# State-times-W1 with two batches in one matmul, its result copied out of PSUM in two halves of 64 partitions

## The chip, the cores and the metric

The kernel runs on one core of one Trainium2 chip. The metric is the device time of one execution in microseconds. TensorE appears in the profile as PE, its weight loads as PEld, VectorE as DVE, ScalarE as ACT, GpSimd as POOL and SyncE as SP.

## The reference

Eight batches of eight heads, 512 positions of 64 values each, are attended to in both directions against a state of 32 rows per head; the result, 544 rows of 512 values per batch, goes through a mixture of eight experts with dense routing. Cut to what matters:

```
scores  = x @ state^T / 8          # softmax over the 32 state rows
xread   = softmax(scores) @ state  # 512 rows per head
sread   = softmax(scores2) @ x     # 32 rows per head, scores2 over the positions
x       = concat(xread, sread)     # 8 batches * 544 rows = 4352 rows of 512
P       = exp(x @ w_gate - max)    # then 8 rounds of row and column scaling
for e in range(8):
    h   = relu(x @ w1[e])          # 512 -> 1024
    out += P[:, e] * (h @ w2[e])   # 1024 -> 512
```

## The kernel before

**Factoring.** For the 512 xread rows of a batch the kernel does not form xread. It keeps the normalised softmax `AT` (for each batch 2 head quads `q` of 128 rows: 4 heads of 32 state rows) and uses `xread @ w1 = A @ (state @ w1)`. So for each batch and expert it first makes `G = state @ w1` (`state_times_w1`, line 210), of 2 quads times 1024 columns, and then `hps = G^T AT` (`layer1`, line 267). The 256 sread rows of all batches are kept as `xs` and go through `w1` directly (line 281).

**State times W1.** `stT_bd` (lines 67 and 133 to 136) holds the transposed state: for each batch and quad 128 columns, of which the 64 of one head pair (`par` 0 or 1) are one stationary operand. The contraction is over the 128 values of a head pair (64 of each of its two heads, block diagonal). A step (q, fh) makes 512 columns of G for one quad with two matmuls of 64 stationary columns each, the even pair into PSUM partitions 0 to 63, the odd one into 64 to 127, and then one copy of 128 partitions into `G` (line 221): on DVE for expert 0, on ACT for the others. There are 4 steps (2 quads, 2 halves of F) for a batch.

**Layer 2.** For expert 0 it is a plain matmul (line 293) whose result ACT copies to `acc` (line 296). For experts 1 to 7 it is a Strassen-Winograd product (`layer2_winograd`, line 304): seven block products per tile on PE (line 333, tiles `ra`, `rb`, `rc`), four sums of hT on DVE in front (lines 316 to 319, tile `sm`), seven scaled additions into `acc` on DVE (line 339), and four differences of W2 blocks for each expert on DVE (`w2_sums`, lines 110 to 113, tile `wt`). `wt` lies in the weight pool of the expert's parity, so two experts' `wt` can live at once.

**Order.** The framework lays out each engine's queue before the program runs, from the order of the source as priority and from what is ready in its own model; an engine then runs its queue in that order. So instructions of neighbouring steps are mixed, and expert 0's work lies among the attention's. In the source, expert 0 runs batch by batch: the four steps for the next batch's G, then the eight `layer1` steps, then four `layer2` steps. Experts 1 to 7 run by pairs of batches `j`: the list `second` (layer 2 of the pair before, 16 steps) is merged with `first` (layer 1 of this pair, 16 steps, with the 4 G steps of a following batch in one lump after the fourth step of each batch). The last pair of an expert has 8 more layer-1 steps for `xs`, and its layer 2, with 4 more steps, is merged into the first pair of the next expert. `w2_sums(e)` stands in the source ahead of that merge.

**Buffers.** PSUM has four banks for attention and four for the experts until expert 0 is done, then eight for the experts. `G` has 2 buffers (one a batch), `hT` 4, `sm` 2.

Of the kernel before, what the change touches and what calls it, by code (L numbers as in the profile page):

```python
# [11 lines left out]
FP16 = mybir.dt.float16  # L12
# [6 lines left out]
def kernel(  # L19
# [9 lines left out]
    nc = tc.nc  # L29

    B, H, S, D = x.shape
# [21 lines left out]
    mh = ctx.enter_context(tc.tile_pool(name="moe_h", bufs=4))  # L53
    mhs = ctx.enter_context(tc.tile_pool(name="moe_hs", bufs=1))
    gsb = ctx.enter_context(tc.tile_pool(name="gate_sb", bufs=2))
    gp = ctx.enter_context(tc.tile_pool(name="gp", bufs=2))

# [6 lines left out]
    Gg = persist.tile([128, B * NQ, E], FP16, name="Gg")  # L64
    Pmat = persist.tile([128, NTB, E], FP32, name="Pmat")
    acc = persist.tile([128, NTB, Dm], FP32, name="acc")
    stT_bd = persist.tile([128, B * NQ, 128], FP16, name="stT_bd")

    w1r = moe_w1.rearrange("e (kc p) f -> e p kc f", p=128)
    w2r = moe_w2.rearrange("e (fb p) d -> e p fb d", p=128)  # L70
# [33 lines left out]

    def w2_sums(e, w2h):

        wt = mw[e % 2].tile([128, 4, FH, DH], FP16, name="wt", tag="wt")
        b11, b12 = w2h[:, :FH, :DH], w2h[:, :FH, DH:]
        b21, b22 = w2h[:, FH:, :DH], w2h[:, FH:, DH:]
        nc.vector.tensor_sub(wt[:, 0], b12, b11)  # L110
        nc.vector.tensor_sub(wt[:, 2], b22, b12)
        nc.vector.tensor_sub(wt[:, 1], b22, wt[:, 0])
        nc.vector.tensor_sub(wt[:, 3], b21, wt[:, 1])
        return wt
# [17 lines left out]
    for g in range(2):  # L132
        t_ps = psA.tile([128, 8, 128], FP16, name="t_ps", tag="a")
        for j in range(8):
            nc.tensor.transpose(t_ps[:, j, :], st_bd[:, 8 * g + j, :], identh)
        nc.vector.tensor_copy(out=stT_bd[:, ds(8 * g, 8), :], in_=t_ps)

    x_nats += [load_x(1), load_x(2)]

    def attention(b):  # L140
        xn = x_nats[b]
        for q in range(NQ):
            bq = b * NQ + q
            xT_ps = psA.tile([128, 2, S], FP16, name="xT_ps", tag="a")
            for par in range(2):
                for sc in range(NSC):
                    nc.tensor.transpose(xT_ps[:, par, ds(128 * sc, 128)],  # L147
                                        xn[:, 2 * q + par, sc, :, :], identh)
            xT = asb.tile([128, 2, S], FP16, name="xT", tag="xT")
            nc.vector.tensor_copy(out=xT, in_=xT_ps)  # L150
            sc_ps = psA.tile([128, S], FP32, name="sc_ps", tag="a")
            for par in range(2):
                nc.tensor.matmul(sc_ps[ds(64 * par, 64), :],  # L153
                                 stT_bd[:, bq, ds(64 * par, 64)], xT[:, par, :])
            E2 = asb.tile([128, S], FP16, name="E2", tag="E2")
            rowsum = asb.tile([128, 1], FP32, name="rowsum", tag="rowsum")
            nc.scalar.activation(out=E2, in_=sc_ps, func=AF.Exp, scale=inv_sqrt_d,
                                 accum_out=rowsum)
            den_ps = psA.tile([128, S], FP32, name="den_ps", tag="a")
            nc.tensor.matmul(den_ps, headones, E2)  # L160
            lnd = asb.tile([128, S], FP32, name="lnd", tag="lnd")
            nc.scalar.activation(out=lnd, in_=den_ps, func=AF.Ln)
            rcp = asb.tile([128, S], FP16, name="rcp", tag="rcp")
            nc.scalar.activation(out=rcp, in_=lnd, func=AF.Exp, scale=-1.0)
            rrec = asb.tile([128, 1], FP32, name="rrec", tag="rrec")
            nc.vector.reciprocal(out=rrec, in_=rowsum)
            En = asb.tile([128, S], FP16, name="En", tag="En")
            nc.vector.tensor_scalar(out=En, in0=E2, scalar1=rrec, scalar2=None, op0=ALU.mult)
            ET_ps = psA.tile([128, NSC, 128], FP16, name="ET_ps", tag="a")
            for sc in range(NSC):  # L170
                nc.tensor.transpose(ET_ps[:, sc, :], En[:, ds(128 * sc, 128)], identh)  # L171
            ET = asb.tile([128, NSC, 128], FP16, name="ET", tag="ET")
            nc.vector.tensor_copy(out=ET, in_=ET_ps)
            nc.vector.tensor_mul(AT[:, q, ds(b * S, S)], E2, rcp)
            su_ps = psA.tile([128, 2, 64], FP32, name="su_ps", tag="a")
            for par in range(2):
                for sc in range(NSC):
                    nc.tensor.matmul(su_ps[:, par, :], xn[:, 2 * q + par, sc, :, :],
                                     ET[:, sc, ds(64 * par, 64)],
                                     start=(sc == 0), stop=(sc == NSC - 1))  # L180
            for i in range(2):
                nc.vector.tensor_copy(
                    out=xs[ds(64 * i, 64), ds(2 * q, 2), ds(b * Ns, Ns)],
                    in_=su_ps[ds(64 * i, 64), :, ds(32 * i, 32)])
# [15 lines left out]
    def state_times_gate():  # L200
        gg_ps = psA.tile([128, B * NQ, E], FP32, name="gg_ps", tag="a")
        for b in range(B):
            for q in range(NQ):
                for par in range(2):
                    nc.tensor.matmul(gg_ps[ds(64 * par, 64), b * NQ + q, :],
                                     stT_bd[:, b * NQ + q, ds(64 * par, 64)],
                                     wgh[:, 2 * q + par, :])
        nc.vector.tensor_copy(out=Gg, in_=gg_ps)

    def state_times_w1(b, w1h, e):  # L210

        evac = nc.vector.tensor_copy if e == 0 else nc.scalar.copy
        G = gp.tile([128, NQ, F], FP16, name="G", tag="G")

        def step(q, fh):
            g_ps = ps["m"].tile([128, 512], FP32, name="g_ps", tag="m")
            for par in range(2):
                nc.tensor.matmul(g_ps[ds(64 * par, 64), :],  # L218
                                 stT_bd[:, b * NQ + q, ds(64 * par, 64)],
                                 w1h[:, 2 * q + par, ds(512 * fh, 512)])  # L220
            evac(out=G[:, q, ds(512 * fh, 512)], in_=g_ps)  # L221

        return G, [partial(step, q, fh) for fh in range(F // 512) for q in range(NQ)]

    for b in range(B):
        if b + 3 < B:
# [7 lines left out]
    actx.close()  # L234
    mw[1] = ctx.enter_context(tc.tile_pool(name="moe_w1", bufs=1))
    sp = ctx.enter_context(tc.tile_pool(name="moe_s", bufs=2))

    for it in range(8):
        rsum = gsb.tile([128, NTB], FP32, name="rsum", tag="rsum")
# [47 lines left out]
    def layer2(e, c, hT, w2h):  # L287

        def step(tk):
            t = c * NSC + tk  # L290
            yps = ps["m"].tile([128, Dm], FP32, name="yps", tag="m")
            for fb in range(NFB):
                nc.tensor.matmul(yps, hT[:, fb, ds(tk * 128, 128)], w2h[:, fb, :],  # L293
                                 start=(fb == 0), stop=(fb == NFB - 1))
            if e == 0:
                nc.scalar.copy(out=acc[:, t, :], in_=yps)
# [73 lines left out]

        return [f for i in range(n) for f in tile_steps(i)]


    w1h, w2h = w_cur
    G_cur, steps = state_times_w1(0, w1h, 0)
    for f in steps:
        f()
    second = []
    for c in range(B + 1):
        if c == 3:  # L380
            w_nxt = load_w(1)
        steps = []
        if c + 1 < B:
            G_nxt, steps = state_times_w1(c + 1, w1h, 0)
        hT, st1 = layer1(c, w1h, G_cur)
        for f in steps + st1:
            f()
        second += layer2(0, c, hT, w2h)
        if c < B - 1:
            for f in second:  # L390
                f()
            second = []
        G_cur = G_nxt

    def merge(a, b):

        k = 0
# [5 lines left out]
        for f in b[k:]:  # L403
            f()

    psctx.close()
    ps["m"] = ctx.enter_context(tc.tile_pool(name="psW", bufs=8, space=bass.MemoryType.PSUM))

    G_nxt, gsteps = state_times_w1(0, w_nxt[0], 1)
    for f in gsteps:
        f()
    for e in range(1, E):
        w1h, w2h = w_nxt
        wt = w2_sums(e, w2h)
        for j in range(B // 2):
            last = j == B // 2 - 1
            first, hs = [], []
            for c in (2 * j, 2 * j + 1):  # L420
                G_cur = G_nxt
                hT, l1 = layer1(c, w1h, G_cur)
                hs.append(hT)
                gs = []
                if c + 1 < B:
                    G_nxt, gs = state_times_w1(c + 1, w1h, e)
                elif e + 1 < E:
                    G_nxt, gs = state_times_w1(0, w_nxt2[0], e + 1)
                first += l1[:4]
                if gs:  # L430
                    first.append(lambda gs=gs: [f() for f in gs])
                first += l1[4:]
            if last:
                hTs, l1 = layer1(B, w1h, None)
                first += l1
# [47 lines left out]
```

## Time and profile before

| | us |
|---|---|
| median of 3 runs | 848.27 (848.17 to 850.55) |
| the profiled execution | 847.74 |
| its span, first to last instruction | 846.0 |
| PE busy in the span | 809.3 |
| DVE busy | 615.7 |
| ACT busy | 474.9 |
| one expert's period in the steady part (from 258.34 to 353.65) | 95.31 |

The profiled execution is 1.7 us longer than its span, which is what lies ahead of the first instruction and behind the last. The first 20 us load x and state; attention with expert 0 runs to about 161 us; then come seven experts; the last 23 us are the last layer 2 and the stores. Matmuls are pipelined and their ends are modelled, so that the busy time of PE counts some waiting; the pieces of the chain of waits, which follow one another without overlap, tell what a group of matmuls adds to the time.

### The profile page before, as it was taken

Reading aid. Unit: us, or ns where it says so; the run is one execution under the profiler, and the core shown is the slowest. Engines: PE = TensorE matmul, PEld = TensorE weight load, DVE = VectorE, ACT = ScalarE, POOL = GpSimd, SP = SyncE. Lnnn points to the kernel's source line nnn. Section 1 sums busy time; section 2 is a strip of 40 time slices with the busy share of each in tenths; the row PEclk is TensorE's granted clock in tenths of the full one; section 3 lists DMA queues with packets and bytes.
Section 4 is the critical chain, followed back from the end, with each engine's and each line's share of the span. In section 5 each row is a group of like instructions: output and inputs, shape, how many; then the busy total and the mean of one; then the engine's idle time right before and its main releaser. Section 6 shows DMA issues by size and latency. Waiting matters only on the chain.

```text
span 846.0 us, 14483 instructions
## 1 busy us (share of the span) xinstructions
PE 809.3 (96%) x5840; PEld 511.3 (60%) x5840; DVE 615.7 (73%) x1320; ACT 474.9 (56%) x908; POOL 41.3 (5%) x67
## 2 busy tenths in 40 slices
PE   0899979999999999999999999999999999999997
PEld 0444434556676666766676666766676666766673
DVE  2656668458777877888777877888777877787763
ACT  0466635775565556555565556555565556555550
POOL 2322010000000000000000000000000000000000
PEclk9999999999999999999999999999999999999999
DMA  9630060330003300230002300230002300002223
GB/s 213 185 101 26 1 100 1 51 51 1 1 1 51 52 1 1 51 50 2 1 1 50 52 1 1 50 51 2 1 1 51 52 1 1 1 13 92 97 97 127
DMA packets 28900, 35.53 MB, mean 42 GB/s; under 512 B 4001, under 2 KB 20385, under 8 KB 28833
## 3 DMA queue, kind: packets, MB, share of 16 engines
q0 software_dynamic: 13328, 16.79, 12.5%
q1 hardware_dynamic: 15504, 17.83, 6.4%
q8 instruction: 45, 0.74, 0.4%
q14 instruction: 23, 0.18, 0.1%
HBM read 42.48 MB, written 8.91 MB: 61 GB/s over the span
## 4 chain that ended last, share of the span: by engine, by line
PE 91%; DVE 4%; DMA 2%; issue 1%; ACT 1%; SPq 0%; POOL 0%; POOLq 0%
PE hps L276 26%; PE ra L333 25%; PE rc L333 12%; PE g_ps L218 8%; PE yps L293 7%; PE rb L333 6%; PE hps L281 3%; DMA x_st<-in_x_dram 2%; DMA w2h<-in_moe_w_dram 1%; DVE G L221 1%; PE sc_ps L153 1%; PE xT_ps L147 1%; DVE xT L150 1%; PE den_ps L160 0%; PE ET_ps L171 0%
## 5 line engine op out<-in xcount | busy, mean ns | idle before, releaser
L283 ACT ACTIVATE hT<-hps 128x512 f16<-128x512 f32 (+1 forms) x576 | 315.4, 577 | 229.8 <-PE hps L276 202.7
L276 PE MATMUL hps<-AT,G 128*128 128x512 f16 x1024 | 286.0, 379 | 3.2 <-DVE G L221 2.1
L339 DVE SCALAR_TENSOR_TENSOR acc<-ra,Pmat,acc 128x256 f32<-128x256 f32 x456 | 216.5, 482 | 51.9 <-PE ra L333 50.8
L333 PEld LDWEIGHTS <-sm 128*128 128x128 f16 x1824 | 173.6, 98 | 77.3 <-issue 9.7
L333 PEld LDWEIGHTS <-hT 128*128 128x128 f16 x1368 | 129.6, 98 | 56.9 <-issue 25.2
L339 DVE SCALAR_TENSOR_TENSOR acc<-rc,Pmat,acc 128x256 f32<-128x256 f32 x228 | 109.9, 482 | 63.9 <-PE rc L333 62.9
L221 ACT CAST G<-g_ps 128x512 f16<-128x512 f32 x224 | 115.6, 599 | 46.0 <-PE g_ps L218 46.0
L333 PE MATMUL ra<-wt,sm 128*128 128x256 f16 x912 | 136.9, 273 | 0.0
L276 PEld LDWEIGHTS <-G 128*128 128x128 f16 x1024 | 98.6, 98 | 58.7 <-issue 14.1
L293 PE MATMUL yps<-w2h,hT 128*128 128x512 f16 x352 | 87.3, 385 | 0.0
L218 PE MATMUL g_ps<-w1h,stT_bd 128*64 128x512 f16 x512 | 84.6, 392 | 0.7 <-ACT hT L283 0.5
L333 PE MATMUL ra<-w2h,hT 128*128 128x256 f16 x456 | 73.1, 273 | 0.0
L333 PE MATMUL rb<-w2h,hT 128*128 128x256 f16 x456 | 69.4, 273 | 0.0
L333 PE MATMUL rc<-wt,sm 128*128 128x256 f16 x456 | 68.6, 273 | 0.0
L333 PE MATMUL rc<-w2h,sm 128*128 128x256 f16 x456 | 68.6, 273 | 0.0
L333 PE MATMUL ra<-wt,hT 128*128 128x256 f16 x456 | 68.5, 272 | 0.0
L339 DVE SCALAR_TENSOR_TENSOR acc<-rb,Pmat,acc 128x256 f32<-128x256 f32 x114 | 54.7, 480 | 5.0
L293 PEld LDWEIGHTS <-hT 128*128 128x128 f16 x352 | 33.2, 100 | 36.3 <-issue 4.2
L218 PEld LDWEIGHTS <-stT_bd 128*64 128x64 f16 x512 | 27.8, 109 | 43.4 <-issue 30.7
L319 DVE TENSOR_TENSOR sm<-hT 128x1024 f16<-128x1024 f16 (+1 forms) x60 | 39.6, 659 | 7.6 <-ACT hT L283 7.6
L316 DVE TENSOR_TENSOR sm<-hT 128x1024 f16<-128x1024 f16 (+1 forms) x60 | 39.4, 657 | 6.9 <-ACT hT L283 6.9
L317 DVE TENSOR_TENSOR sm<-sm,hT 128x1024 f16<-128x1024 f16 (+1 forms) x60 | 39.3, 655 | 0.0
(142 smaller groups left out, 401.2 us busy)
## 6 DMA issues: line engine op xcount, KB each, us to landing
x_st<-in_x_dram SPq DMA_DIRECT2D x16, 512.0 KB, 4.6
w1h<-in_moe_w_dram POOLq DMA_DIRECT2D x16, 512.0 KB, 7.0
w2h<-in_moe_w_dram POOLq DMA_DIRECT2D x16, 512.0 KB, 7.4
out_dram<-acc SPq DMA_DIRECT2D x32, 256.0 KB, 2.3
st_nat<-in_state_dram SPq DMA_DIRECT2D x1, 512.0 KB, 3.9
out_dram<-acc SPq DMA_DIRECT2D x8, 64.0 KB, 1.7
wgh<-in_moe_w_gate_dram POOLq DMA_DIRECT2D x1, 8.0 KB, 4.4
```

The costliest lines, as they stand in the source:

```text
L147: nc.tensor.transpose(xT_ps[:, par, ds(128 * sc, 128)], xn[:, 2 * q + par, sc, :, :], identh)
L218: nc.tensor.matmul(g_ps[ds(64 * par, 64), :], stT_bd[:, b * NQ + q, ds(64 * par, 64)], w1h[:, 2 * q + par, ds(512 * fh, 512)])
L221: evac(out=G[:, q, ds(512 * fh, 512)], in_=g_ps)
L276: nc.tensor.matmul(hps[:, :tn], G[:, q, ds(fb * 128, 128)], AT[:, q, ds(c * S, S)], start=(q == 0), stop=(q == NQ - 1))
L281: nc.tensor.matmul(hps[:, :tn], w1h[:, kc, ds(fb * 128, 128)], xs[:, kc, :], start=(kc == 0), stop=(kc == NKC - 1))
L283: nc.scalar.activation(out=hT[:, fb, :], in_=hps[:, :tn], func=AF.Relu)
L293: nc.tensor.matmul(yps, hT[:, fb, ds(tk * 128, 128)], w2h[:, fb, :], start=(fb == 0), stop=(fb == NFB - 1))
L316: nc.vector.tensor_add(s1, a21, a22)
L317: nc.vector.tensor_sub(s2, s1, a11)
L319: nc.vector.tensor_sub(s3, a11, a21)
L333: nc.tensor.matmul(r[nm], a[:, k, ds(128 * i, 128)], b[:, k, :], start=(first and k == 0), stop=(k == FH - 1), skip_group_check=True)
L339: nc.vector.scalar_tensor_tensor(out=dst, in0=r[nm], scalar=Pmat[:, t + i, e:e + 1], in1=dst, op0=ALU.mult, op1=ALU.add)
```

## The change

One matmul now takes the same head pair of two batches as its 128 stationary columns. `stT` is laid out as [batch pair, head pair `kc`, half, 64]. In even batches the even head pair sits in half 0 and the odd one in half 1; in odd batches they are swapped, so that the two batches never want the same half of a head pair. In attention the score rows of odd batches swap halves accordingly, and with them `AT`, `ET` and `Gg`. A step (kc, fh) is one matmul of 128 x 512, followed by two copies of 64 partitions, each into the G of its batch: on ACT and DVE for expert 0, both on ACT for the others. A pair of batches has 8 steps where it had 8 steps of two matmuls and one copy. `G` has 4 buffers. To make room, `wt` moves out of the two weight pools into one pool with one buffer for all experts. `stT` is filled by four smaller copies per group, two on ACT and two on DVE, instead of one on DVE. In expert 0 the G steps of the next pair are merged among the layer-1 and layer-2 steps of the odd batch, and the copies of `acc` from batch 5 on go to DVE. In experts 1 to 7 the G steps are no longer lumped: one follows every second layer-1 step.

```diff
-    gp = ctx.enter_context(tc.tile_pool(name="gp", bufs=2))
+    gp = ctx.enter_context(tc.tile_pool(name="gp", bufs=4))
...
-    stT_bd = persist.tile([128, B * NQ, 128], FP16, name="stT_bd")
+    stT = persist.tile([128, B // 2, NKC, 2, 64], FP16, name="stT")
...
-        wt = mw[e % 2].tile([128, 4, FH, DH], FP16, name="wt", tag="wt")
+        wt = wtp.tile([128, 4, FH, DH], FP16, name="wt", tag="wt")
...
-        nc.vector.tensor_copy(out=stT_bd[:, ds(8 * g, 8), :], in_=t_ps)
+        t_v = t_ps.rearrange("p (a b q) (h n) -> p a b q h n", b=2, q=NQ, h=2)
+        for par in range(2):
+            for odd in range(2):
+                (nc.vector.tensor_copy if odd else nc.scalar.copy)(
+                    out=stT[:, ds(2 * g, 2), par::2, par ^ odd, :], in_=t_v[:, :, odd, :, par, :])
...
-                nc.tensor.matmul(sc_ps[ds(64 * par, 64), :],
-                                 stT_bd[:, bq, ds(64 * par, 64)], xT[:, par, :])
+                nc.tensor.matmul(sc_ps[ds(64 * (par ^ odd), 64), :],
+                                 stT[:, b // 2, 2 * q + par, par ^ odd, :], xT[:, par, :])
...
-                                     ET[:, sc, ds(64 * par, 64)],
+                                     ET[:, sc, ds(64 * (par ^ odd), 64)],
...
-    def state_times_w1(b, w1h, e):
-
-        evac = nc.vector.tensor_copy if e == 0 else nc.scalar.copy
-        G = gp.tile([128, NQ, F], FP16, name="G", tag="G")
-
-        def step(q, fh):
+    def state_times_w1(bp, w1h, e):
+
+        G = [gp.tile([128, NQ, F], FP16, name="G", tag="G") for _ in range(2)]
+
+        def step(kc, fh):
             g_ps = ps["m"].tile([128, 512], FP32, name="g_ps", tag="m")
-            for par in range(2):
-                nc.tensor.matmul(g_ps[ds(64 * par, 64), :],
-                                 stT_bd[:, b * NQ + q, ds(64 * par, 64)],
-                                 w1h[:, 2 * q + par, ds(512 * fh, 512)])
-            evac(out=G[:, q, ds(512 * fh, 512)], in_=g_ps)
-
-        return G, [partial(step, q, fh) for fh in range(F // 512) for q in range(NQ)]
+            nc.tensor.matmul(g_ps, stT[:, bp, kc, :, :], w1h[:, kc, ds(512 * fh, 512)])
+            for half in range(2):
+                evac = nc.vector.tensor_copy if e == 0 and half else nc.scalar.copy
+                evac(out=G[half ^ (kc % 2)][ds(64 * half, 64), kc // 2, ds(512 * fh, 512)],
+                     in_=g_ps[ds(64 * half, 64), :])
+
+        return G, [partial(step, kc, fh) for fh in range(F // 512) for kc in range(NKC)]
...
+    wtp = ctx.enter_context(tc.tile_pool(name="moe_wt", bufs=1))
...
-                nc.scalar.copy(out=acc[:, t, :], in_=yps)
+                (nc.scalar.copy if c < B - 3 else nc.vector.tensor_copy)(out=acc[:, t, :], in_=yps)
...
+    Gs, steps = state_times_w1(0, w1h, 0)
...
+        G = None if c == B else Gs[c % 2]
+        steps = []
+        if c % 2 and c + 1 < B:
+            Gs, steps = state_times_w1(c // 2 + 1, w1h, 0)
+        hT, st1 = layer1(c, w1h, G)
+        second += layer2(0, c, hT, w2h)
+        if c < B - 1:
+            merge(st1 + second, steps)
+            second = []
+        else:
+            merge(st1, steps)
...
+            G = Gs
+            if not last:
+                Gs, gs = state_times_w1(j + 1, w1h, e)
+            elif e + 1 < E:
+                Gs, gs = state_times_w1(0, w_nxt2[0], e + 1)
             for c in (2 * j, 2 * j + 1):
...
+                hT, l1 = layer1(c, w1h, G[c % 2])
                 hs.append(hT)
...
+                for k in range(NFB):
+                    first.append(l1[k])
+                    if k % 2:
+                        first += gs[4 * (c % 2) + k // 2:][:1]
```

More of the change, by code (lines that the diff above doesn't have):

```diff
@@ L141, in attention @@
         xn = x_nats[b]
+        odd = b % 2
         for q in range(NQ):
-            bq = b * NQ + q
             xT_ps = psA.tile([128, 2, S], FP16, name="xT_ps", tag="a")
@@ L204, in state_times_gate @@
                 for par in range(2):
-                    nc.tensor.matmul(gg_ps[ds(64 * par, 64), b * NQ + q, :],
-                                     stT_bd[:, b * NQ + q, ds(64 * par, 64)],
+                    half = par ^ (b % 2)
+                    nc.tensor.matmul(gg_ps[ds(64 * half, 64), b * NQ + q, :],
+                                     stT[:, b // 2, 2 * q + par, half, :],
                                      wgh[:, 2 * q + par, :])
         nc.vector.tensor_copy(out=Gg, in_=gg_ps)
-    def state_times_w1(b, w1h, e):
-        evac = nc.vector.tensor_copy if e == 0 else nc.scalar.copy
-        G = gp.tile([128, NQ, F], FP16, name="G", tag="G")
-        def step(q, fh):
+    def state_times_w1(bp, w1h, e):
+        G = [gp.tile([128, NQ, F], FP16, name="G", tag="G") for _ in range(2)]
+        def step(kc, fh):
             g_ps = ps["m"].tile([128, 512], FP32, name="g_ps", tag="m")
-            for par in range(2):
-                nc.tensor.matmul(g_ps[ds(64 * par, 64), :],
-                                 stT_bd[:, b * NQ + q, ds(64 * par, 64)],
-                                 w1h[:, 2 * q + par, ds(512 * fh, 512)])
-            evac(out=G[:, q, ds(512 * fh, 512)], in_=g_ps)
-        return G, [partial(step, q, fh) for fh in range(F // 512) for q in range(NQ)]
+            nc.tensor.matmul(g_ps, stT[:, bp, kc, :, :], w1h[:, kc, ds(512 * fh, 512)])
[4 more added lines that the diff above has]
+        return G, [partial(step, kc, fh) for fh in range(F // 512) for kc in range(NKC)]
     for b in range(B):
@@ L371, in layer2_winograd @@
         return [f for i in range(n) for f in tile_steps(i)]
[L374 to L393, printed above, removed]
     def merge(a, b):
@@ L404, in merge @@
             f()
+    w1h, w2h = w_cur
+    Gs, steps = state_times_w1(0, w1h, 0)
+    for f in steps:
+        f()
+    second = []
+    for c in range(B + 1):
+        if c == 3:
+            w_nxt = load_w(1)
+        G = None if c == B else Gs[c % 2]
[6 more added lines that the diff above has]
+            merge(st1 + second, steps)
+            second = []
+        else:
+            merge(st1, steps)
     psctx.close()
     ps["m"] = ctx.enter_context(tc.tile_pool(name="psW", bufs=8, space=bass.MemoryType.PSUM))
-    G_nxt, gsteps = state_times_w1(0, w_nxt[0], 1)
+    Gs, gsteps = state_times_w1(0, w_nxt[0], 1)
     for f in gsteps:
@@ L419 @@
             first, hs = [], []
+            gs = []
+            G = Gs
[3 more added lines that the diff above has]
+                Gs, gs = state_times_w1(0, w_nxt2[0], e + 1)
             for c in (2 * j, 2 * j + 1):
-                G_cur = G_nxt
-                hT, l1 = layer1(c, w1h, G_cur)
+                hT, l1 = layer1(c, w1h, G[c % 2])
                 hs.append(hT)
[L424 to L432, printed above, removed]
+                for k in range(NFB):
+                    first.append(l1[k])
+                    if k % 2:
+                        first += gs[4 * (c % 2) + k // 2:][:1]
             if last:
```

## The prediction

> **What bounds the kernel now.** First the page: who is busy, and along what the chain of waits runs.
>
> ```profile
> PE 809.3 (96%) x5840; PEld 511.3 (60%) x5840; DVE 615.7 (73%) x1320; ACT 474.9 (56%) x908; POOL 41.3 (5%) x67
> PE 91%; DVE 4%; DMA 2%; issue 1%; ACT 1%; SPq 0%; POOL 0%; POOLq 0%
> PE hps L276 26%; PE ra L333 25%; PE rc L333 12%; PE g_ps L218 8%; PE yps L293 7%; PE rb L333 6%; PE hps L281 3%; DMA x_st<-in_x_dram 2%; DMA w2h<-in_moe_w_dram 1%; DVE G L221 1%; PE sc_ps L153 1%; PE xT_ps L147 1%; DVE xT L150 1%; PE den_ps L160 0%; PE ET_ps L171 0%
> ```
>
> The chain is 91% PE, and the matmuls that the change touches (line 218) are 8% of it. Shares are averages, so next the view of busy time by stretch, for one expert's period and for the end of expert 0.
>
> ```profile
> 258.34:353.65 95.31, 95.31 (x703) 64.17 (x704) 75.71 (x160) 55.69 (x104) 2.91 (x4) 1.00 0.14 23
> 144.00:161.00 17.00, 16.88 (x94) 9.10 (x93) 12.07 (x30) 12.27 (x28) 0.00 (x0) 1.00 0.00 0
> 161.00:175.00 14.00, 13.65 (x70) 6.01 (x70) 1.84 (x4) 11.02 (x23) 1.41 (x2) 1.00 0.46 77
> ```
>
> The columns are length, then PE, PEld, DVE, ACT, POOL busy, clock, DMA. In a period of 95.31 us PE is never idle at a full clock; DVE has 19.6 us free and ACT 39.6 us. There are seven such periods, so this stage is decided by PE's time alone. What the G matmuls cost there is read from the chain of waits in order of time (start, length, what), whose pieces do not overlap. Its head for the period, then two stretches:
>
> ```profile
> by line: PE ra L333 33.0%; PE hps L276 29.2%; PE rc L333 16.4%; PE g_ps L218 10.3%; PE rb L333 7.9%; PE hps L281 3.7%
> ...
> 258.34 0.98 PE g_ps L218 x8
> ...
> 292.89 0.55 PE g_ps L218 x3
> ...
> 293.98 0.77 PE g_ps L218 x5
> ...
> 336.13 0.98 PE g_ps L218 x8
> ```
>
> ```profile
> 270.57 0.44 PE ra L333 x4
> 271.00 0.98 PE g_ps L218 x8
> 271.99 0.54 PE ra L333 x4
> ```
>
> ```profile
> 278.27 0.86 PE hps L276 x4
> ...
> 280.92 0.33 PE g_ps L218
> 281.25 0.54 PE rc L333 x4
> 281.80 0.44 PE ra L333 x4
> 282.23 0.98 PE g_ps L218 x7
> ```
>
> Three things are to be seen. A full matmul of 512 columns adds 0.215 us (four in 0.86). Of the 64-column ones a lone one adds 0.33, and seven add 0.98, no more than eight do: the further six or seven came as three more streams of (0.98 - 0.33) / 3 = 0.217 us, two matmuls side by side in each. So the even and odd pair already share a stream, and one full matmul for them is no gain by itself. The gain is elsewhere. Going into the 64-column form costs 0.33 - 0.215 = 0.115 us, and coming out 0.10 (four line-333 matmuls take 0.54 instead of 0.44). And where the queue separates one matmul from its partner (1 + 7, or 3 + 5), eight matmuls take five streams instead of four.
>
> **PE's side of the change.** A period has eight batches' blocks: three whole (0.98 us, the rows at 258.34 and 336.13 are the first and last), four split 1 + 7 (0.33 + 0.98 = 1.31) and one split 3 + 5 (0.55 + 0.77 = 1.32): 2.94 + 5.24 + 1.32 = 9.50 us in 13 pieces (10.3% of 95.31 is 9.8; it holds one piece of the next period). With 13 x 0.10 for coming out: 10.8 us. After: 32 matmuls of the form of line 276, 32 x 0.215 = 6.9 us, with no form to change, and nothing to split. Gain 3.9 us a period, **27.4 us in seven**. PE's period would be 91.4 us. The page's rule that speaks against this stands with the rivals.
>
> Expert 0 has eight such blocks too, at the same price at most 3.9 us. In the first of them PE is waiting for other things anyway, so I take **2.5** (0 to 3.9).
>
> **The copies out of PSUM.** Per period 32 copies become 64 of half the partitions.
>
> ```profile
> L283 ACT ACTIVATE hT<-hps 128x512 f16<-128x512 f32 (+1 forms) x72 | 39.8, 575 | 32.9 <-PE hps L276 29.1 <-PE hps L281 3.6
> ...
> L221 ACT CAST G<-g_ps 128x512 f16<-128x512 f32 x32 | 16.5, 598 | 6.8 <-PE g_ps L218 6.8
> ```
>
> ```profile
> L221 DVE CAST G<-g_ps 128x512 f16<-128x512 f32 x32 | 21.2, 678 | 0.5
> L296 ACT COPY acc<-yps 128x512 f32<-128x512 f32 x34 | 19.8, 584 | 31.2 <-PE yps L293 30.8
> ...
> L150 DVE COPY xT<-xT_ps 128x1024 f16<-128x1024 f16 x16 | 11.1, 692 | 3.0 <-PE xT_ps L147 2.7
> ...
> L173 DVE COPY ET<-ET_ps 128x512 f16<-128x512 f16 x16 | 6.8, 424 | 6.0 <-PE ET_ps L171 6.0
> ...
> L130 DVE CAST st_bd<-st_nat 32x1024 f16<-32x1024 f32 x4 | 2.7, 683 | 0.0
> ...
> L89 DVE CAST x_nat<-x_st 128x512 f16<-128x512 f32 x4 | 1.5, 424 | 13.6 <-DMA x_st<-in_x_dram 13.6
> ```
>
> No ACT row has 64 partitions. DVE's rows show what counts: 32 partitions of 1024 elements take 683 ns, 128 of 512 take 424. Fewer partitions bring nothing, so I take the full price, 16.5 / 32 = 0.516 us busy (bounds: half of it, 0.26, if size alone counted; 0.60, the mean of one without overlap). ACT then has 39.8 + 64 x 0.516 = 72.8 us of work in 91.4, 80%; PE stays the bound on average. The last pair of an expert is denser: while the 12 tile steps of layer 2 of three tiles run (28 matmuls each, 0.44 / 4 = 0.109 us apiece: 9.2 us) with 16 layer-1 steps (16 x 0.43 = 6.9) and 8 G steps (1.7), PE needs 17.8 us, and ACT 16 x 39.8/72 (0.55) + 16 x 0.516 = 17.1 us, or 19.2 at 0.60 each. The eight steps for `xs` behind it give room again. So 0 to 1.4 us a period; I take 0.43, **3.0 in seven**. Copies that come late hold a PSUM bank, of eight, and behind them in ACT's queue wait the hT activations, for which PE's next pair waits. DVE, in expert 0, keeps 32 half copies, and gets the 14 copies of `acc` from batch 5 on: 14 x 0.678 = 9.5 us, of which the two stretches shown have 4.9 and 12.2 us of DVE idle time; cost 0, and if that cover failed at most those 9.5 us. ACT loses 14 x 0.584 and gets 32 x 0.516 there, spread over 140 us.
>
> `stT` is filled in eight pieces of 256 columns in place of two of 1024: on DVE about 0.29 us each (0.692 and 0.424 give 0.052 us per 100 columns), on ACT like it. In parallel nothing is lost (4 x 0.29 against 2 x 0.692); if ACT and DVE took turns on a bank, 2.3 us against 1.4. Cost 0 to 0.9, taken **0.4**.
>
> **The one buffer of wt.** Between experts the four differences of line 110 to 113 now wait for the last reader of the old `wt`, and the next pair's layer 2 waits for them. The timeline at that place, a period before:
>
> ```profile
> 277.02 0.60 PE L333 MATMUL ra<-wt,hT 128*128 128x256 f16 x4
> ...
> 277.54 0.69 DVE L316 TENSOR_TENSOR sm<-hT 128x1024 f16<-128x1024 f16 x1 [0.58 <-ACT hT L283]
> ...
> 278.55 0.68 DVE L317 TENSOR_TENSOR sm<-sm,hT 128x1024 f16<-128x1024 f16 x1
> ...
> 278.98 0.60 PE L333 MATMUL rc<-wt,sm 128*128 128x256 f16 x4
> ```
>
> The last reader ends at 277.6; `rc`, the first to need the new `wt`, starts at 278.98. Four operations on DVE started one after another take about 0.61 each (277.54 to 278.15 was one), 2.4 us in all, just when DVE makes the sums for the same products; queued behind them are these sums and the additions that free PSUM banks. The work itself is not new: before, it ran earlier in the expert. PE has layer-1 steps to put in between. So 0 to 2.4 us at six boundaries; I take 0.7, **4.2**. The weights' DMAs and their places in POOL's queue are unchanged.
>
> **The sum**, against the profiled execution of 847.74: -27.4 - 2.5 + 3.0 + 0.4 + 4.2 = -22.3, so 825.4. The median of the runs shown is 0.5 above that execution: **826**.
>
> **Rivals.**
> 1. All covers hold, and a stall of expert 0 goes with the new order. The chain has it:
>
> ```profile
> 106.65 6.14 DMA w2h<-in_moe_w_dram
> 112.79 3.66 issue
> 116.45 0.69 DVE wt L110
> ```
>
> DVE's queue reached `w2_sums(1)` before the weights had landed, and PE idled with it. Without it and without the three losses: 848.3 - 27.4 - 3.9 - 3.7 = 813. Against: nothing in the diff moves this load.
>
> 2. ACT is the bound in each last pair, or each lone copy costs 0.60, and bunched copies hold banks: the 1.4 us in full and as much in the other pairs: 7 x 2 - 3 = 11 more, 837.
>
> 3. The `wt` wait is bare at each boundary: 6 x 2.4 - 4.2 = 10 more, 836.
>
> 4. No gain: the two half-matmuls shared a stream already (217 ns), and the cost at the pieces' edges belongs to any change of operands and stays; then only the splits' extra streams go, 5 x 0.215 x 7 = 7.5 us, and the three losses (7.6) eat them: 848. Against: between lines 276 and 333 the same chain shows no such edges. The Trainium skill, TensorE: Matmul & The Clock Gate, Measured speedup vs the span model, has packed column tiles run side by side at some 4 ns extra each; the trace agrees (217 against 215). By that alone 224 full matmuls in place of 448 halves would save about 1 us, an estimate by that page, and this rival would be the likeliest.
>
> 5. Slower: a half copy on ACT costs far more than a whole one did. ACT outlasts the old period from 39.8 + 64 p = 95.31, p = 0.87 us; at 1 us it would be 103.8 a period, +8.5 x 7: 908. For it stands that no row has the form, against it the DVE rows. The Trainium skill, TensorEngine Tiling (Array Packing), PSUM Bottleneck, advises both ScalarE and VectorE for copies out of PSUM; after the change all 64 of a period are on ACT, which no run here shows yet.
>
> **How the numbers follow.** Forecast 826 (818 to 833 by itself): 0.62. Rival 1: 0.15. Rival 2: 0.09. Rival 3: 0.06. Rival 4: 0.04. Rival 5: 0.04. The range from 812 to 840 holds all but the last two, and the worst of 2 and 3 together. A measurement of this kernel tells about 0.3% from no change, 2.5 us: faster 0.92, same 0.04, slower 0.04.
>
> **What would show it.** Right: a period of 91 to 93 us with PE busy throughout; pieces of line 218's successor at 0.215 each, and 0.44 behind them; ACT near 73 us a period with half copies near 0.52; wt's differences just behind the boundary. Wrong: PE waits for `hT` or `G` from ACT (rival 2, 5), line 333's weight loads waiting for DVE's `wt` (3), matmuls of 0.33 (4). An order of the queues that splits or bunches steps in a way that the source does not tell would shift the losses by some microseconds each way.

## The result and the profile after

| | before | after |
|---|---|---|
| median, us | 848.22 (848.16 to 850.55) | 829.09 (828.66 to 829.91) |
| ratio to before | | 0.9769, 95% interval 0.975 to 0.9788 |
| profiled execution / its span, us | 847.74 / 846.0 | 828.78 / 826.9 |

The changed kernel is 19.1 us faster; 826 was forecast, in a range of 812 to 840. Line numbers shift by a few: state-times-W1 is now line 223 (matmul) and 226 (copies), layer 1 line 283 and 290, Winograd line 340, its additions line 346. First the page: busy time, and the chain by engine and by line.

```profile
PE 783.3 (95%) x5584; PEld 518.3 (63%) x5584; DVE 621.1 (75%) x1336; ACT 613.0 (74%) x1154; POOL 41.4 (5%) x67
PE 82%; DVE 8%; ACT 5%; DMA 3%; issue 1%; POOL 0%; SPq 0%
PE ra L340 24%; PE hps L283 23%; PE rc L340 12%; PE yps L300 6%; PE rb L340 5%; PE g_ps L223 5%; PE hps L288 3%; ACT G L226 2%; DMA x_st<-in_x_dram 2%; DVE G L226 2%; ACT hT L290 2%; DMA w2h<-in_moe_w_dram 1%; PE xT_ps L153 1%; DVE xT L156 1%; PE sc_ps L159 1%
```

The G matmuls fell from 8% to 5% of the chain, ACT's busy time rose from 474.9 to 613.0 us, and more of the chain now lies on the copying engines: DVE's part went from 4% to 8%, ACT's from 1% to 5%. Where, is told by the busy time in two stretches: a period in the steady part, and the stretch from expert 0's `xs` matmuls to expert 1's (columns as in the prediction).

```profile
251.19:342.69 91.50, 91.37 (x670) 65.14 (x668) 74.80 (x159) 74.24 (x138) 2.91 (x4) 1.00 0.15 24
160.63:251.19 90.56, 86.71 (x565) 54.67 (x564) 57.92 (x121) 81.97 (x154) 2.91 (x4) 1.00 0.15 24
```

The period went from 95.31 to 91.50 us with PE busy throughout. In the other stretch PE idles 3.9 us and ACT is busy for 82.0 of 90.6 us. The chain in order of time shows the pieces that the change was about:

```profile
262.68 0.44 PE rb L340 x4
263.12 0.22 PE g_ps L223
263.33 0.44 PE rc L340 x4
```

One full matmul adds 0.22 us and the four behind it take 0.44, not 0.54: both edges (going into the 64-column form and coming out of it) are gone.

The kernel cut at five marks (end of attention: the start of its last gate matmul; then the start of each expert's first `xs` matmul, line 281 before, 288 after), in us:

| stage | before | after | difference |
|---|---|---|---|
| up to the end of attention | 105.8 | 106.8 | +1.0 |
| from there to expert 0's xs | 51.5 | 53.8 | +2.3 |
| to expert 1's xs | 88.0 | 90.6 | +2.6 |
| five periods, experts 2 to 6 | 476.6 | 457.5 | -19.1 |
| to expert 7's xs | 94.4 | 88.4 | -6.0 |
| the rest | 29.8 | 29.8 | 0 |

Two of these rows exchange work: the eight G steps of an expert's first pair now all run in the expert before it, where four of them did before. So expert 1's row holds more G steps than before and expert 7's fewer; the two go together. The first two rows are of single executions, which differ from each other by 1 us and more (experiments 6 and 9 to 11).

### The profile page after: what moved, and what is told of

Read it like the earlier page. It is cut to its first block, busy times and chain, and to the rows that moved or that the text cites. A ratio compares the mean times of both kernels' runs of the same rounds, so it can differ in the third digit from the quotient of the medians.

```text
span 826.9 us, 14183 instructions
## 1 busy us (share of the span) xinstructions
PE 783.3 (95%) x5584; PEld 518.3 (63%) x5584; DVE 621.1 (75%) x1336; ACT 613.0 (74%) x1154; POOL 41.4 (5%) x67
## 4 chain that ended last, share of the span: by engine, by line
PE 82%; DVE 8%; ACT 5%; DMA 3%; issue 1%; POOL 0%; SPq 0%
PE ra L340 24%; PE hps L283 23%; PE rc L340 12%; PE yps L300 6%; PE rb L340 5%; PE g_ps L223 5%; PE hps L288 3%; ACT G L226 2%; DMA x_st<-in_x_dram 2%; DVE G L226 2%; ACT hT L290 2%; DMA w2h<-in_moe_w_dram 1%; PE xT_ps L153 1%; DVE xT L156 1%; PE sc_ps L159 1%
## 5 line engine op out<-in xcount | busy, mean ns | idle before, releaser
L290 ACT ACTIVATE hT<-hps 128x512 f16<-128x512 f32 (+1 forms) x576 | 307.3, 573 | 86.3 <-PE hps L283 50.0
L226 ACT CAST G<-g_ps 64x512 f16<-64x512 f32 x480 | 277.1, 578 | 54.0 <-PE g_ps L223 50.5
L346 DVE SCALAR_TENSOR_TENSOR acc<-ra,Pmat,acc 128x256 f32<-128x256 f32 x456 | 215.8, 481 | 54.3 <-PE ra L340 53.7
L340 PEld LDWEIGHTS <-sm 128*128 128x128 f16 x1824 | 177.2, 98 | 71.5 <-issue 7.7
L340 PEld LDWEIGHTS <-hT 128*128 128x128 f16 x1368 | 133.4, 97 | 52.6 <-issue 8.7
L223 PE MATMUL g_ps<-w1h,stT 128*128 128x512 f16 x256 | 96.1, 382 | 2.1 <-DVE G L226 1.4
L340 PE MATMUL ra<-w2h,hT 128*128 128x256 f16 x456 | 70.7, 273 | 0.0
L300 PEld LDWEIGHTS <-hT 128*128 128x128 f16 x352 | 33.6, 100 | 36.8 <-issue 4.3
L325 DVE TENSOR_TENSOR sm<-hT,sm 128x1024 f16<-128x1024 f16 (+1 forms) x60 | 39.4, 656 | 0.2
```

Of the source, the lines that this page charges most:

```text
L223: nc.tensor.matmul(g_ps, stT[:, bp, kc, :, :], w1h[:, kc, ds(512 * fh, 512)])
L226: evac(out=G[half ^ (kc % 2)][ds(64 * half, 64), kc // 2, ds(512 * fh, 512)], in_=g_ps[ds(64 * half, 64), :])
L290: nc.scalar.activation(out=hT[:, fb, :], in_=hps[:, :tn], func=AF.Relu)
L325: nc.vector.tensor_sub(s4, a12, s2)
L340: nc.tensor.matmul(r[nm], a[:, k, ds(128 * i, 128)], b[:, k, :], start=(first and k == 0), stop=(k == FH - 1), skip_group_check=True)
L346: nc.vector.scalar_tensor_tensor(out=dst, in0=r[nm], scalar=Pmat[:, t + i, e:e + 1], in1=dst, op0=ALU.mult, op1=ALU.add)
```

## The experiments

Each kernel is timed against the kernel before on the same chip, where that kernel had a median of 848.03 us (experiments 1 to 4), 848.25 (5 to 8) or 848.19 (9 to 12); so times of different groups can be compared.

**1. The full matmul alone.** In the kernel before, one matmul per step:

```diff
-            for par in range(2):
-                nc.tensor.matmul(g_ps[ds(64 * par, 64), :],
-                                 stT_bd[:, b * NQ + q, ds(64 * par, 64)],
-                                 w1h[:, 2 * q + par, ds(512 * fh, 512)])
+            nc.tensor.matmul(g_ps, stT_bd[:, b * NQ + q, :],
+                             w1h[:, 2 * q, ds(512 * fh, 512)])
```

> The kernel before, with one change: each step of state-times-W1 is one full matmul of 128 stationary columns (both head pairs of the batch against the W1 rows of the even pair; the odd pair's W1 rows are left out, so half of G is other numbers), still one copy of 128 partitions, same lumps, same buffers. Theory (the gain is on PE alone: edges of the 64-column form and half-matmuls that lost their partner): the seven expert periods fall from 95.3 to 91.4-91.6 us each, expert 0 by 1 to 4 us, in all 817 to 821 us, some 8 to 12 us better than the changed kernel's 829.1. Rival (the gain comes from spreading the G steps and from G's four buffers): no change, 846 to 849 us.

Measured 819.76 us, ratio 0.9658 (0.9634 to 0.9683). A period:

```profile
239.80:331.36 91.56, 91.56 (x670) 64.91 (x669) 74.99 (x160) 55.46 (x104) 2.91 (x4) 1.00 0.14 24
```

PE alone gives 28.3 us, without any other part of the change: expert 1's row -4.1, the five periods -18.8, expert 7's -3.5, expert 0 with attention -1.4. All that the change does besides costs some 9 us (829.1 against 819.8). By the marks of the profiled executions 4.8 us lie ahead of expert 0's xs and 3.8 behind.

**2. The old matmuls, spread.** In the kernel before, the lump is taken apart:

```diff
-                first += l1[:4]
-                if gs:
-                    first.append(lambda gs=gs: [f() for f in gs])
-                first += l1[4:]
+                for k in range(NFB):
+                    first.append(l1[k])
+                    if k % 2:
+                        first += gs[k // 2:][:1]
```

> The kernel before, with its two 64-column matmuls and one copy per step, but in experts 1 to 7 the G steps are spread as in the changed kernel, one after every second layer-1 step. Theory: every step now is a piece with two edges of its own, 0.33 + 0.10 us instead of 0.215: 32 x 0.43 = 13.9 us in place of 10.8 a period, so 98 to 99 us a period and 865 to 872 us in all. Rival (spreading by itself helps): below 846 us.

Measured 868.65 us, ratio 1.0232 (1.0211 to 1.0253); a period is 98.23 us. The chain shows the price of each piece:

```profile
262.54 0.44 PE rb L333 x4
262.98 0.34 PE g_ps L218 x2
263.31 0.54 PE rc L333 x4
```

Two halves together take 0.34 us and make the matmuls behind them 0.10 longer, 0.44 in all against 0.22 for one full matmul. That is 0.22 more for each of 32 steps, 7.0 us a period; on 91.5 us it gives 98.5. With halves, spreading costs 20 us; the lumps of the old kernel kept the number of edges down.

**3. One copy in place of two.** In the changed kernel, for experts 1 to 7:

```diff
+            if e > 0:
+                nc.scalar.copy(out=G[kc % 2][:, kc // 2, ds(512 * fh, 512)], in_=g_ps)
+                return
```

> The changed kernel, but in experts 1 to 7 the result of a step is copied by one ACT instruction of 128 partitions into one of the two G tiles, instead of two of 64 partitions into both (the swap of halves is left out, so G holds the wrong batch's rows in half of its places). Theory (the doubled copies cost only where ACT is full, from 165 to 192 us, when expert 1 starts): the steady period stays at 91.3 to 91.5 us, the stretch between expert 0's and expert 1's xs matmuls falls from 90.6 to 86.5-87.5 us, in all 825 to 826.5 us. Rival (the copies cost 0.43 us in every period as the prediction had it): 822 to 823 us, with periods near 91.0.

Measured 824.4 us, ratio 0.9713 (0.9692 to 0.9734). The same two stretches as above:

```profile
248.48:339.93 91.45, 91.32 (x671) 65.16 (x669) 75.00 (x160) 55.94 (x105) 2.91 (x4) 1.00 0.14 24
162.28:248.48 86.20, 85.59 (x566) 54.93 (x564) 58.19 (x122) 59.28 (x115) 2.92 (x4) 1.00 0.15 25
```

In the steady period 18.3 us of ACT's work goes and the time stays (91.45 against 91.50). In the stretch of expert 1 it gives 4.4 us. So in experts 1 to 7 the doubled copies cost time only there; expert 0 keeps its half copies in this kernel. The timelines of that place, first before, then after:

```profile
162.12 2.05 ACT L221 CAST G<-g_ps 128x512 f16<-128x512 f32 x4 [0.82 <-PE g_ps L218]
```

```profile
164.76 1.89 PE L223 MATMUL g_ps<-w1h,stT 128*128 128x512 f16 x8 [0.47 <-ACT hT L290]
165.17 9.55 ACT L226 CAST G<-g_ps 64x512 f16<-64x512 f32 x16 [0.46 <-PE g_ps L223]
...
169.99 0.61 PE L283 MATMUL hps<-AT,G 128*128 128x512 f16 x2 [0.82 <-ACT G L226]
```

The changed source makes G for two batches ahead of expert 1's layer 1: 16 copies, 9.55 us on ACT, where four copies took 2.05. PE waits for G, and ACT carries on at full load: from 165 to 192 us it is busy for 26.3 of 27 us, while PE idles 3.4.

**4. One wt buffer alone.** In the kernel before:

```diff
-        wt = mw[e % 2].tile([128, 4, FH, DH], FP16, name="wt", tag="wt")
+        wt = wtp.tile([128, 4, FH, DH], FP16, name="wt", tag="wt")
...
+    wtp = ctx.enter_context(tc.tile_pool(name="moe_wt", bufs=1))
```

> The kernel before, with wt in one pool with one buffer for all experts. Theory (the wait at an expert's boundary is nearly hidden by layer-1 matmuls): 0 to 0.3 us at each of six boundaries, 848 to 850 us. The prediction's term: 0.7 each, 852.4 us. The bare wait: 2.4 each, 862 us.

Measured 847.21 us, ratio 0.9985 (0.9968 to 1.0001); a period is 95.0 us, not longer. The wait costs nothing here. Nor does it show in the changed kernel, whose period (91.50 us, one buffer) is no longer than that of experiment 1 (91.56, two).

**5. Half of expert 1's first copies on DVE.** In the changed kernel:

```diff
-                evac = nc.vector.tensor_copy if e == 0 and half else nc.scalar.copy
+                evac = nc.vector.tensor_copy if half and (e == 0 or (e == 1 and bp < 2)) else nc.scalar.copy
```

> The changed kernel, but for the first two pairs of batches of expert 1 the upper halves of state-times-W1 go to DVE instead of ACT. Theory (after expert 0 ACT alone sets the pace from 165 to 192 us, because 16 half copies for expert 1 stand ahead of its layer-1 results): ACT loses 16 copies of 0.59 us there, DVE has the room, the stretch between the xs matmuls of expert 0 and 1 falls from 90.6 to 86-87.5 us, all others stay: 825 to 826 us. Rival (the stretch is long because of the seam between the PSUM pools or because of layer 2 of expert 0): unchanged, 828 to 830.

Measured 824.8 us, ratio 0.9717 (0.969 to 0.9744). The stretch is 86.74 us, with 68.31 us of DVE and 72.10 of ACT. This confirms from the other side what experiment 3 showed: it is ACT's load, not the seam between the PSUM pools or expert 0's layer 2.

**6. Expert 0's copies by step.** In the changed kernel, both halves of a step on one engine:

```diff
-                evac = nc.vector.tensor_copy if e == 0 and half else nc.scalar.copy
+                evac = nc.vector.tensor_copy if e == 0 and kc % 2 else nc.scalar.copy
```

> The changed kernel, but in expert 0 both half copies of a step go to the same engine, ACT for the even head pairs and DVE for the odd ones, instead of the lower half to ACT and the upper one to DVE. Theory (DVE's half copy waits for ACT's on the same bank, and PE then for DVE's, in 20-30 and 130-138 us; the idle time at 20-30 brings the clock of 0.66 in 30-40 us): attention's second batch starts 1 to 1.7 us earlier and the xs matmuls of expert 0 begin at 157 to 159 instead of 160.6 us; in all 826 to 828 us. Rival (the cost is the doubled number of copies, whoever makes them): no change, 828.5 to 830.

Measured 830.5 us, ratio 0.9787 (0.9767 to 0.9808). This lies outside both expectations. The stretch behind attention is 53.6 us, and attention itself ended 3 us later, at a granted clock of 0.50 where experiment 5, with the changed kernel's own expert 0, had 1.00. First experiment 5, then this one, at 38 to 42 us:

```profile
38.00:42.00 4.00, 4.00 (x36) 2.11 (x35) 1.78 (x6) 3.58 (x9) 0.00 (x0) 1.00 0.74 251
```

```profile
38.00:42.00 4.00, 4.00 (x22) 1.69 (x20) 0.69 (x1) 2.24 (x7) 0.00 (x0) 0.50 0.76 261
```

The theory that ACT and DVE taking turns on a bank is what costs in expert 0 is not borne out: executions that keep the change's own copies there differ from each other by more (53.8 us with the change, 54.3 in experiment 5, 55.4 in experiment 3). The 1.0 us up to the end of attention goes with the clock: experiments 5 and 8, whose attention and expert 0 up to there are the changed kernel's, kept a clock of 1.00 and ended it at 105.9 us, the profiled run of the change at 106.8, after a clock of 0.69 over 30 to 34 us and 0.50 over 34 to 38. So at a full clock the changed attention is no slower. But it may make such a dip of the clock likelier: six of the nine profiled executions with the changed attention had one between 31 and 43 us, and none of the five with the old attention, which ended at 105.4 to 106.1 us. No run decides this.

**7. Expert 1's differences of W2 on GpSimd.**

```diff
-        nc.vector.tensor_sub(wt[:, 0], b12, b11)
+        eng = nc.gpsimd if e == 1 else nc.vector
+        eng.tensor_sub(wt[:, 0], b12, b11)
...
```

> The changed kernel, but the four differences of W2 for expert 1 alone run on GpSimd instead of DVE. Theory (in expert 0 DVE stands at these differences until the weights have landed, the scaling rounds behind them wait, and PE idles for 5.1 us at 118.7-123.7 and then runs at a lower clock): the stall goes, the xs matmuls of expert 0 begin 3 to 6 us earlier, in all 823 to 826 us. Rival (PE waits there for the scaling rounds themselves): within 1 us of 829.1.

Measured 826.4 us, ratio 0.9736 (0.9716 to 0.9757): the stretch behind attention fell from 53.8 to 50.7 us, and expert 0's xs began 2.2 us earlier, less than the 3 to 6 expected. PE's one idle stretch of 5.1 us is gone, but three of 1.0 to 1.6 us came in its place. The timeline shows what was in the way:

```profile
118.12 2.12 POOL L113 TENSOR_TENSOR wt<-w2h 128x1024 f16<-128x1024 f16 x1 [7.51 <-DVE cpart L253]
...
118.72 1.82 DVE L258 SCALAR_TENSOR_TENSOR Pmat<-crec,Pmat 128x272 f32<-128x272 f32 x1
```

The DVE operation beside GpSimd's takes 0.44 us elsewhere, here 1.82.

**8. The acc copies back on ACT.**

```diff
-                (nc.scalar.copy if c < B - 3 else nc.vector.tensor_copy)(out=acc[:, t, :], in_=yps)
+                nc.scalar.copy(out=acc[:, t, :], in_=yps)
```

> The changed kernel, but all copies of expert 0's results into acc go to ACT as before (14 of them back from DVE). Theory (these copies are not what made expert 0 longer: the first on DVE runs at 140 us, after the long wait; and ACT is full from 165 us on): the xs matmuls of expert 0 begin at 159.5 to 161 us as with the change, and the stretch after them gets 2 to 5 us longer: 831 to 834 us. Rival (they delay the scaling rounds and so expert 0): xs matmuls at 157 to 158 us, 825 to 827 us in all.

Measured 833.52 us, ratio 0.9821 (0.9801 to 0.9842). Expert 0's xs began at 160.4 us as with the change, and the stretch after it took 95.1 us instead of 90.6. So this part of the change is worth 4.4 us, and the reason that fits is that of experiments 3 and 5: ACT is full there.

**9 to 11. The differences of W2 late.** For expert 1 they are queued on DVE behind the last scaling round; in the changed kernel, in the kernel before, and in the changed kernel together with experiment 5:

```diff
-        nc.vector.scalar_tensor_tensor(out=Pmat,
+        scaled = nc.vector.scalar_tensor_tensor(out=Pmat,
...
-        wt = w2_sums(e, w2h)
+        with (tc.issue_after(scaled.ins) if e == 1 else ExitStack()):
+            wt = w2_sums(e, w2h)
```

> The changed kernel, but the four differences of W2 for expert 1 are queued on DVE behind the last of the eight scaling rounds, instead of among them. Theory (DVE stands at them until the weights land, and PE behind the scaling rounds; on GpSimd the stall went, but DVE's rounds were stretched beside it, 1.82 us for an operation of 0.44): PE's idle time at 118-124 us falls from 5.1 to under 1.5 us, the stretch from the end of attention to expert 0's xs matmuls from 53.8 to 48-50.5 us; in all 823 to 826 us. Rival (PE waits for the rounds themselves): within 1 us of 829.1.

> The kernel before with the same edit. Theory (the stall is the old kernel's too, 3.85 us there, and the change only made it 1.3 us longer): 843 to 846 us, the stretch from attention's end to the xs matmuls from 51.5 to 47.5-49.5 us. Rival (the old order hides it): 847.5 to 849 us.

> The changed kernel with both edits: the differences for expert 1 behind the last scaling round, and for the first two pairs of expert 1 the upper halves copied by DVE. Theory: the two stretches are apart, so the gains add: 829.1 less 4.3 (e1_dve) less 3 to 6: 819 to 822 us, below both kernels. Rival (the differences, late, meet the copies on DVE after 165 us): 823 to 826 us.

Measured 821.28 us, ratio 0.9682 (0.9665 to 0.9699); 842.12, ratio 0.9929 (0.9915 to 0.9944); and 817.5, ratio 0.9638 (0.9621 to 0.9654). All three are faster than their expectations had it. The chain of the changed kernel at this place, which the edit undoes:

```profile
108.91 11.73 DMA w2h<-in_moe_w_dram
120.65 0.02 issue
120.67 0.69 DVE wt L113
...
123.13 0.55 DVE cpart L252
123.68 0.04 issue
123.72 0.59 PE csb_ps L254 x2
124.31 4.05 PE yps L300 x12
```

DVE waits for the weights, the scaling round behind it is late, and PE, whose queue holds the round's small matmul, has not one instruction from 118.7 to 123.7 us. The twelve matmuls after it take 4.05 us, 0.34 each instead of 0.215. The kernel before has a stall of 3.7 us, but another one. There PE waits from 114.0 to 117.7, and the sum that it waits for (`cpart`) stands behind the first difference alone, which started at 116.45; the second difference, which needs the later half of the weights, came behind that sum. The timeline of DVE in the kernel before:

```profile
116.45 0.69 DVE L110 TENSOR_TENSOR wt<-w2h 128x1024 f16<-128x1024 f16 x1 [3.66 <-issue]
117.06 0.63 DVE L245 TENSOR_REDUCE cpart<-Pmat 128x8 f32<-128x272 f32 x1
118.93 0.69 DVE L111 TENSOR_TENSOR wt<-w2h 128x1024 f16<-128x1024 f16 x1 [1.25 <-DMA w2h<-in_moe_w_dram]
```

In the changed kernel the `cpart` that PE waits for stands behind the second to fourth differences (lines 113 to 115), so PE waits for the later half of the weights, and the difference that waits for that half also started 1.7 us later (120.67 against 118.93). The stretch from attention to the xs matmuls, with the edit in the changed kernel and in the one before:

| | as it was | differences late |
|---|---|---|
| before | 51.5 | 46.5 |
| after | 53.8 | 47.4 |

So 1.4 of the 2.3 us that the change loses in this stretch are this stall, longer than the old one; 0.9 us is left, and the 1.2 us that experiment 1 gained in the same stretch (50.25 against 51.46) do not show either. These are single executions; experiments 9 and 11 agree here (47.4 us both), the stalled ones differ by up to 1.6 us. The third kernel beats both kernels and each edit alone: the gains of 7.8 and 4.3 us, which the edits had one by one, nearly add up, to 11.6 us.

**12. The full matmuls in lumps.** In the changed kernel:

```diff
-                for k in range(NFB):
-                    first.append(l1[k])
-                    if k % 2:
-                        first += gs[4 * (c % 2) + k // 2:][:1]
+                first += l1[:4]
+                first += gs[4 * (c % 2):][:4]
+                first += l1[4:]
```

> The changed kernel, but in experts 1 to 7 four G steps stand in one lump after the fourth layer-1 step of each batch, as before, instead of one after every second step. Theory (without the edges of the 64-column form the place of the steps costs PE nothing): periods of 91.4 to 92 us, 828.5 to 832 us. Rival (the spreading is what keeps ACT's eight half copies in a row from holding PSUM banks): over 92.5 us a period, 836 us and more.

Measured 849.82 us, ratio 1.0025 (1.001 to 1.004). My theory falls, and the rival holds: the period is 94.69 us, and the whole gain is lost. The busy time of that period, then two lines of the waits, and the timeline before one of them:

```profile
252.62:347.31 94.69, 91.56 (x670) 64.87 (x668) 75.30 (x160) 74.33 (x137) 2.91 (x4) 1.00 0.14 23
```

```profile
PEld L340 <- DVE sm L323: 25.8, 21, 2.7
...
DVE sm L323 <- ACT hT L290: 14.1, 21, 1.9
```

```profile
277.05 4.76 ACT L226 CAST G<-g_ps 64x512 f16<-64x512 f32 x8 [0.49 <-PE g_ps L223]
...
281.83 1.09 ACT L290 ACTIVATE hT<-hps 128x512 f16<-128x512 f32 x2
```

PE has the same work as in the changed kernel and now idles 3.1 us a period. Eight half copies in a row hold ACT for 4.76 us; the hT activations stand behind them, the sums on DVE wait for hT, and PE's weight loads wait for the sums (25.8 us in all; 2.2 in the changed kernel). By these rows it is ACT's order that ties PE, not, as the expectation had it, PSUM banks that ACT holds: the waits of layer 1's matmuls that a G copy of ACT ended come to 1.0 us, against 1.6 in the changed kernel. (Waits of PE for DVE's additions, which free banks, come to 6.0 us.) With one copy per step, as in experiment 1, lumps did no harm: there four copies make a lump.

## Why the prediction was right, and where it was off

**PE's gain.** 27.4 us in seven periods and 2.5 in expert 0 were forecast; experiment 1 has 26.4 and 1.4. This is the mechanism as forecast: a period of 91.50 us where 91.4 was worked out, with the pieces at 0.22 and 0.44. Experiment 2, where every half has its partner beside it, shows the edges by more of them. At its price, 0.22 for both edges, the 13 pieces of an old period make 2.8 of the 3.75 us that experiment 1 gains a period; the rest fits the five streams without a partner (5 x 0.215 = 1.1), an estimate that no run tested by itself. Rival 4 (the edges are nobody's) is out.

**The doubled copies on ACT.** The price was near: 277.1 us for 480 half copies, 0.577 each, against 0.516 taken and 0.60 as the upper end. The place where they cost was wrong. The forecast had 0.43 us in each period, at the dense last pair; by experiment 3 the periods lost 0.05. It had nothing for the start of expert 1, where 16 copies now stand ahead of layer 1, and this cost 4.4 us. I had counted ACT's load over a period and in the densest pair, not at the one place where the change puts eight steps in front of everything.

**The spreading** was in the diff and I gave it no term. Rival 2 named bunched copies, at 11 us, and its sum does not follow from its words: 1.4 us and as much again are 2.8 a period, 7 x 2.8 - 3 = 16.6 more, which is 843 and outside the range. In the changed kernel ACT's copies in the steady part come in twos, and this rival did not come; in experiment 12 they come in eights, and the whole kernel is 20.7 us slower. The spreading is what makes the two copies affordable.

**The wait for wt**: 4.2 us forecast, nothing measured (experiment 4), so rival 3 is out. The row that I used showed DVE's 2.4 us and the 1.4 us until the first use. The prediction named the cover, PE's layer-1 matmuls in between, but took 0.7 us as left over at each boundary; that it covers all of it fits the time, and no run took the cover away.

**Expert 0**: the forecast had -2.5 and +0.4, the table has +3.3. Of this 1.0 goes with the dip of the clock in the profiled execution (experiment 6), and 1.4 is the stall at expert 1's differences of W2, which the prediction saw in the trace and priced only as a chance of gain (rival 1). It got longer: the sum that PE waits for now stands behind the differences that need the later half of the weights, and the first of these also started later. Left are 0.9 us, and the 1.4 us of PE's gain that did not show; whether they are the half copies or the new order was not told apart.

Rival 5, the slower one, is out: no half copy on ACT took more than 0.61 us, against its 0.87. Together the losses were 9.3 us instead of 7.6, and the gain 28.3 instead of 29.9: 3 us off 826. The gain is near because its mechanism was right. That the sum of the losses is near is luck. The term of 3.0 came as 4.4 at another place, that of 4.2 came to nothing, and where 0.4 was forecast for expert 0 the change lost 4.8 us against experiment 1: 1.2 up to the end of attention, 1.4 by the longer stall, neither of which had a term, and some 2 us that stay unexplained. The errors nearly cancelled.

## What to carry to other kernels

Before filling a half-used stationary operand, read what the halves cost in the chain: here they shared a stream, and only the edges of the form and lone halves were to be won. A result copied out in two halves by one engine doubled here what that engine spends on them (18.3 us more a period, on 16.5); it was free only while the copies were spread and the engine had room, so look at every place where a loop starts up and several steps stand in front. A weight preparation that an engine's queue meets before its weights have landed stops all that is queued behind it: put it behind the last urgent work.

## What the runs showed of the hardware that was not expected

- **Half copies on ACT do not overlap.** In the lump of 16 above, they start 9.55 / 16 = 0.60 us apart, while one takes 0.58; four whole copies in a row before took 2.05 us with 0.60 for the last, so 0.48 apart. In such a row a half copy costs 2.5 times as much per element as a whole one.
- **DVE beside GpSimd**: one operation of 0.44 us took 1.82 while GpSimd ran a subtraction (experiment 7), and GpSimd took 2.1 us for what DVE does in 0.69. The Trainium skill, SBUF — State Buffer, Who interferes with whom, has the two share a pair of SBUF ports under an exclusive lock; the trace agrees with a stretching of that kind, and does not show the lock itself.
- **The clock after an idle stretch**: behind the 5.1 us without a matmul, PE's granted clock was 0.74 over 124 to 130 us, and twelve matmuls cost 1.5 us extra. In experiment 9, without that stall, it stayed at 1.00; in experiment 10 it was 1.00 over 118 to 124 us, where the kernel before, behind its own stall, had 0.72. At the kernel's start the same code met clocks between 0.50 and 1.00 (over 34 to 38 us, the changed kernel's own execution against experiment 5), and attention ended at 106.8 and 105.9 us. The stretch behind the stall in the changed kernel, then the same time in experiment 9:

```profile
124.00:130.00 6.00, 6.00 (x24) 2.69 (x25) 3.90 (x10) 1.34 (x3) 0.00 (x0) 0.74 0.00 0
```

```profile
124.00:130.00 6.00, 4.84 (x20) 1.73 (x19) 5.68 (x11) 5.81 (x12) 0.00 (x0) 1.00 0.00 0
```
